# One core, 20,241 instructions: a top-k attention and two feed-forward blocks, replanned with other costs for landings, transposes and a shared port

## The chip, the cores and the metric

The kernel runs on one core of a Trainium2 chip. The metric is the device time of the program in microseconds. Three runs of the kernel before took 990.5, 990.6 and 991.75 us, so the median is 990.6 us. The execution that was profiled took 994.35 us, of which the span from the first to the last instruction is 992.6 us.

Five engines work side by side, each in the fixed order of its own instructions: PE (matrix products), DVE (VectorE), ACT (ScalarE), POOL (GpSimd) and SP, which does no arithmetic and issues all DMAs. An instruction that waits for a semaphore holds up everything behind it on its engine.

## The reference

```python
# attention: q, k, v are 4 x 8 x 576 x 64
scores = scale * np.matmul(q, k.transpose(0, 1, 3, 2))
kth = np.partition(scores, -32, axis=-1)[..., -32:-31]
scores = np.where(scores >= kth, scores, -1000000000.0)
scores = scores - np.max(scores, axis=-1, keepdims=True)
attn = np.exp(scores)
attn = attn / (np.sum(attn, axis=-1, keepdims=True) + 1e-09)
x = np.matmul(attn, v)            # as 2304 tokens x 512
# first block: w_in 512 x 2048, w_out 2048 x 512
h = x @ w_in
x = (h * (1.0 / (1.0 + np.exp(-1.702 * h)))) @ w_out
# second block: w1, w2 512 x 1024, w3 1024 x 1024, w_out 1024 x 512
out = ((x @ w1) * (x @ w2)) @ w3 @ w_out
```

The weights come in float64. Products are made in float16 with a high and a low half of each operand, three matmuls for one product (lines 789 to 791).

## The kernel before, in words

**Tiles and heads.** The 2304 tokens are 18 tiles of 128; a tile has 8 heads, so there are 144 heads. For one head PE makes the scores of 128 tokens with 576 keys into one of two score banks (`s_ps`, L1127, "S" below). DVE finds the 32 largest in four rounds of MAX8 (L1147) with three MATCH_REPLACE8 between them (L1150). ACT cuts (L1165, which also frees the score bank) and takes the exponential (L1168). ACT or POOL makes the high half ("a hi", L1174 or L1228), POOL or DVE the low half in two pieces ("a lor", 64 columns, L1177, and "a lo", 512 columns, L1180). A DMA transpose turns both halves into one of two `ats` buffers ("a T", L1183), and PE multiplies them with v ("av", L1195 and L1199).

**The two blocks.** After 8 heads a tile runs through `moe`: x is split and transposed ("x T", L1286), four products with w_in ("h"), tanh and gate (L1344 to L1356, "g"), split (L1313 to L1319) and transposed ("g T", L1359), products with w_out ("x2"), split and transposed ("x2 T", L1412), products with w1 and w2 ("a", "b"), their product p (L1461 or L1467), split and transposed ("p T", L1493), the product with w3 times w_out, made once at the start ("o"), and the store (L1509).

**The weights.** In the first 200 us 72 blocks of 512 KB are loaded (L483), rebuilt from their 64-bit words (ACT or POOL at L488, L493, L498 and L515, ACT at L503, DVE at L507), measured (PE at L551) and split (L598 to L630). K and v of each batch are prepared ahead of its tiles.

**What sets the order.** The code first records 5339 operations, each with one or more ways of doing it (an engine and a cost). A table of numbers (`PLAN`) gives each operation its rank and its way. `Order.run` goes through them by rank and emits each on its engine; it keeps modelled times only to choose which free buffer an operation gets. So the order on each engine, SP's DMA queue among them, is that of the table, and the semaphores follow from what each instruction reads and writes.

Buffers in the row of names below: `usb`, `tsb`, `psb` and `ysb` are rings in SBUF, `mm` are four PSUM banks, `w`, `win` and `wout` hold weights.

Of the kernel before, what the change touches and what calls it, by code (L numbers as in the profile page):

```python
# [21 lines left out]
P = 128  # L22
C = 512
# [14 lines left out]
class Order:  # L38
    GAP = {"T": 0.25, "V": 0.16, "A": 0.16, "G": 0.1, "D": 0.05, "N": 0.0}
    SAME = {"T": 0.0, "V": 0.12, "A": 0.12, "G": 0.1, "D": 0.25, "N": 0.0}  # L40
    DMA = 2.1
    COLD = ((50.0, 1.28), (100.0, 1.03))
# [99 lines left out]
    'c-jq@W1A(t0!2$nC8?w;N!3{A^f^6k_t-N%wr$(CZQHhO+qP}%oqPYm{;;3D)>af%(G{rJN@^vG;`8~HJW5_AzhWpr!3t5h!jv>hCdKomQUXe>66Oo_rBgzb'  # L142
    'cqKteRthWCl{!iRUqN4zl3U5A6jLhu8u{Az+WAT<6@9yv`btA(lrmMB>-*)~9C9>dy0Th1t6WhYDKC|`zE{d`<&W}3`R6OBwpaQp!<CWB4CTJ>r*DLRoU&ZG'
    'p*&VzD_@l#itVrEpXiVG=T<MMoz#WuGIhDST0QJP;TIuK)lYt;2%l73CB2eX$>7WEi%_DJvPuPCC0}i&sZvxa?yI6yRaz+-m8`ySU!0Od(G=5X`KaP3)s&jP'
    'TE1pVS0$)K`l5X~l_E+<Wr%O6Z<exEX{~he4OYe~)0DbOJ*9!tMCqZ-QRXXqlmp5^rKd99w@^8*oKRXQEq&dULCR!hnX<vR$+uV8ubfoQD;JcD%4OxMa?O`j'
    '4Oe5;C&~-o2Srh#`d!gg<R@x6)l!+C`xDh1Y6-Qb+DL7owp7!oq5cRpuUbsaqQ>|W{JGS!YH_u^zn;H|+EgvAlvg?^os@1$FQvEAPZ^*LR7NOclnKgAWuvmC'
    '!J!668cZy>NLjD!R3<6sd{caveDeyfQPwK!l)D8#DxZ{Z%It#Ml*P(+Wu<aU*{s}FR`^ym*wJ8DgMG>|<&1J&xvAVy?kNwHhssmsx$;JNr@U8&s1wwc>Kb*e'
    'x=vlMZculthtyN*dG(t5Ks8mVW>N!coSIWr{YD|z@A>nn`P9;C8MU0MsaO?iDz%haM-BSJ)M$Spe`~da+D+}Fj#6v;>#Ftrjs5-Afoev-uaMs#;vcHcP?xAn'
    ')y-;Ge~&`F{bT*d)Jy7ob%nZBy`p|o|EQX#Ylim5|5p9%|LTv_qBNxO!ct48<<|;mr9vu(R1V3ig%{4IW!GA0Z8fa9nx_S{f!ZK#lr~<Qs+9|=rd1EA6*5;_'
    't<BVC7hbF_*S2a0wL{ti?U7bTYg4#`)>nI|ebzQ<I}7jC4roZnx~)5U27QmZ-+$15S-q-8soDJb)rx90wXNFD-&q~4PFMS?1JvQ_ICYkKR6Xv$qyANiHb@<;'  # L150
    'j#1~T^VCV|Wd9ETUiGxvOl|IO@9(H~QKzVj{2SGq>PPjgde{HT|3Uqw{#H%R3Q4O4wG3JoEli8ia%vCNcj`~o)*Nk^I?_L0y{_I+Q)wAPVzp!~ueLy2sI3Xv'
    'rk&Rwsn68s>I?Oys%WYPwbWX)mZ@;lM!rUq8<p0|Hfq?YNuxA{>kX<sXxN}cEl;DQMl~Cq)y`>`w9DER?Va{s`=}{8(RDp3;0E#q78O~puhKW`S@bwPR?ng5'
    '*GmRU1*!+0YrnML+JD+Vjq9GCUJvRqdP0!`fn0&wfuZ_ZeYU<%57l$)QF=i=LeHy5>P2*^r_wX(ne;F{Tu;=q={fa6dR@Jx-a+rASJfNpZS=PKM15mmQeab{'
    'T#@>L%7F%fP%R>)Q%F~>x7J+i9MUbMpEg08rp*bNAF@>2s1??VYIQ@}Y3;RqTA`34S_!R^R$ptN^$!`WjnPJEW3}laGqhP+cdduE=l{iF`VsAv_C@=vnfi9^'
    'SjerAXWAQWnYJQieaLR@q;^<49&$qarm6a4Ekq9lD(Thqi(2+TdA+9IT(75h)cXed=`;18TC+eeeXu@9Z?AXOyXal@Zh8;BzdleOrH|9c>l5^8`Ye5}K3`v~'
    'uh!S->-DYrZvBjYF>obtBk;ONY%nocDELax5KI@$8r-X&&=2S*^#^(`BiYDp9MMk)jt1@ruIYCIw*yZD--;MUMx&rn+Ncw(9jq5TR^*|6PJgM>lt{xd;*32-'
    '{slnL3cf2+ESM=+Hh8GWt;RPSKWf~^m|*lZCL2mh(V!hH9xSY<1R4bz>%H|?TD*Q%zpFpf%j&HHWArWhWqp7?Jg_0~RsW;=jOs>1qq)(}$ZTXWqKpzo1>>Wh'
# [1410 lines left out]
```

## Time and profile before

| | |
|---|---|
| median of three runs | 990.6 us |
| profiled execution | 994.35 us, span 992.6 us |
| PE busy | 942.2 us (95%) |
| DVE busy | 901.7 us (91%) |
| POOL busy | 832.5 us (84%) |
| ACT busy | 730.0 us (74%) |
| DMA engines, mean busy share of queue 1 | 72.3% |

Busy time is the time in which an engine has at least one instruction under way. PE's matmuls overlap: a 128x512 matmul shows 0.38 us from start to end, and the next one starts 0.22 us after it. A wait that is shorter than this overlap leaves no idle time in the profile. A wait is put down to the releaser that came last.

### The profile page before, as it was taken

How to read it: one execution, taken by the hardware profiler on the slowest of the kernel's cores; microseconds unless marked ns; L12 is line 12 of the kernel's file. 1: busy time of each engine (PE TensorE's matmuls, PEld its weight loads, DVE VectorE, ACT ScalarE, POOL GpSimd, SP SyncE). 2: the span in 40 equal slices, each digit the busy share in tenths (PEclk: the TensorE clock that was granted, in tenths of full speed). 3: DMA queues.
4: the chain of work that ended last, by engine and by line, in shares of the span. 5: the costliest groups of instructions: out<-in, count | busy, mean ns of one | idle time of the engine just before them, and what ended most of it. 6: DMA issues, size and time to landing. Idle time of an engine off the chain costs nothing. (4 is left out here: it accounts for less than half of the span.)

```text
span 992.6 us, 20241 instructions
## 1 busy us (share of the span) xinstructions
PE 942.2 (95%) x6790; PEld 495.7 (50%) x6790; DVE 901.7 (91%) x1939; ACT 730.0 (74%) x1369; POOL 832.5 (84%) x1180
## 2 busy tenths in 40 slices
PE   5688879899999999999999999999999999999998
PEld 2445544445455555545555555545455555555544
DVE  6999999899999999999999999999999999999422
ACT  7999989896877787877688776776785775646241
POOL 6889999898899999999999999988897878757142
PEclk9699999999999999999999999999999999999999
DMA  9999988876788887767887868669666667555401
GB/s 322 291 280 291 277 179 191 173 135 131 122 149 151 155 156 136 134 130 152 146 158 139 147 129 147 121 127 165 127 126 134 113 118 117 111 90 102 99 11 33
DMA packets 398569, 149.37 MB, mean 150 GB/s; under 512 B 376576, under 2 KB 384768, under 8 KB 398464
## 3 DMA queue, kind: packets, MB, share of 16 engines
q1 hardware_dynamic: 398464, 148.07, 72.3%
q8 instruction: 53, 0.87, 0.4%
q14 instruction: 52, 0.43, 0.1%
HBM read 52.43 MB, written 4.72 MB: 58 GB/s over the span
## 5 line engine op out<-in xcount | busy, mean ns | idle before, releaser
L1147 DVE MAX8 m8s<-ysb 128x8 f32<-128x576 f32 x432 | 320.5, 752 | 5.7
L1150 DVE MATCH_REPLACE8 ysb<-m8s,ysb 128x576 f32<-128x576 f32 x288 | 213.6, 742 | 0.0
L1180 POOL TENSOR_TENSOR ysb<-ysb 128x512 f16<-128x512 f32 x141 | 163.8, 1166 | 0.3
L1165 ACT ACTIVATE ysb<-s_ps,m8s 128x576 f32<-128x576 f32 x144 | 106.7, 741 | 77.5 <-DVE m8s L1147 72.5
L789 PE MATMUL mm<-w,usb 128*128 128x512 f16 x388 | 147.1, 379 | 1.2 <-POOL usb L1319 1.0
L791 PE MATMUL mm<-w,usb 128*128 128x512 f16 x388 | 147.0, 379 | 0.0
L790 PE MATMUL mm<-w,usb 128*128 128x512 f16 x388 | 147.0, 379 | 0.0
L791 PEld LDWEIGHTS <-usb 128*128 128x128 f16 x912 | 89.1, 98 | 107.8
L789 PEld LDWEIGHTS <-usb 128*128 128x128 f16 x912 | 89.0, 98 | 100.2 <-issue 7.0
L1168 ACT ACTIVATE ysb<-ysb,nbs,asm 128x576 f32<-128x576 f32 x144 | 124.5, 867 | 17.0 <-DVE nbs L1157 8.5
L790 PEld LDWEIGHTS <-usb 128*128 128x128 f16 x912 | 89.1, 98 | 91.3 <-issue 2.1
L789 PE MATMUL mm<-wout,usb 128*128 128x512 f16 x304 | 115.3, 379 | 1.7 <-DMA usb<-usb 0.6
L791 PE MATMUL mm<-wout,usb 128*128 128x512 f16 x304 | 115.2, 379 | 0.0
L790 PE MATMUL mm<-wout,usb 128*128 128x512 f16 x304 | 115.2, 379 | 0.0
L1147 DVE MAX8 m8s<-s_ps 128x8 f32<-128x576 f32 x144 | 108.6, 754 | 6.2 <-PE s_ps L1127 3.4
L1150 DVE MATCH_REPLACE8 ysb<-m8s,s_ps 128x576 f32<-128x576 f32 x144 | 107.5, 747 | 0.0
L1127 PE MATMUL s_ps<-kts,qts 128*128 128x288 f16 (+1 forms) x640 | 96.4, 290 | 2.5 <-ACT ysb L1165 2.2
L789 PE MATMUL mm<-win,usb 128*128 128x512 f16 x220 | 83.5, 379 | 0.6 <-DMA usb<-usb 0.6
L791 PE MATMUL mm<-win,usb 128*128 128x512 f16 x220 | 83.4, 379 | 0.0
L790 PE MATMUL mm<-win,usb 128*128 128x512 f16 x220 | 83.4, 379 | 0.0
L1195 PE MATMUL mm<-v2s,ats 128*128 128x65 f16 (+1 forms) x1440 | 79.1, 194 | 3.4 <-DMA ats<-ysb 2.7
L1195 PEld LDWEIGHTS <-ats 128*128 128x128 f16 (+1 forms) x1440 | 73.5, 100 | 12.4 <-DMA ats<-ysb 3.8
(369 smaller groups left out, 2131.3 us busy)
## 6 DMA issues: line engine op xcount, KB each, us to landing
w<-in_moe_w_out_dram SPq DMA_DIRECT2D x24, 512.0 KB, 5.5
w<-in_moe_w_dram SPq DMA_DIRECT2D x22, 512.0 KB, 5.7
w<-in_moe_w_in_dram SPq DMA_DIRECT2D x16, 512.0 KB, 6.0
qts<-qts SPq DMA_DIRECT2D x34, 128.0 KB, 2.6
out_dram<-usb SPq DMA_DIRECT2D x17, 256.0 KB, 2.3
usb<-in_q_dram SPq DMA_DIRECT2D x15, 256.0 KB, 3.4
usb<-in_v_dram SPq DMA_DIRECT2D x11, 256.0 KB, 3.1
usb<-in_k_dram SPq DMA_DIRECT2D x10, 256.0 KB, 3.3
```

The lines of the kernel that those rows point to most:

```text
L789: nc.tensor.matmul(o, a[:, i, :], hi, start=(first and i == 0), stop=False)
L790: nc.tensor.matmul(o, a[:, i, :], lo, start=False, stop=False)
L791: nc.tensor.matmul(o, a[:, 4 + i, :], hi, start=False, stop=(last and i == 3))
L1127: nc.tensor.matmul(E["sp"][r : r + n, i], qe[q_][:, h, r : r + n], kt[:, j, i * HS : (i + 1) * HS], start=k_ == 0, stop=k_ == 1,)
L1147: nc.vector.max(out=E["m8"][:, 8 * i : 8 * i + 8], in_=E["sp"] if i == 0 else E["w"])
L1150: nc.vector.match_replace(out=two(E["w"]) if i == 0 else E["w"], in_to_replace=E["m8"][:, 8 * i : 8 * i + 8], in_values=E["sp"] if i == 0 ...
L1165: nc.scalar.activation(two(E["y"]), E["sp"], AF.Prelu, bias=E["m8"][:, TOPK - 1 : TOPK], scale=-1.0, alpha=1.0 / FAR)
L1168: nc.scalar.activation(E["y"], E["y"], AF.Exp, bias=E["nb"], scale=nesc)
L1180: return lambda: eng.tensor_tensor(hl()[:, S + SR : 2 * S], E["y"][:, 0:SM], hl()[:, 0:SM], op=ALU.subtract)
L1195: nc.tensor.matmul(heads_av()[r : r + n, j_, 0 : D + 1], at_, v2[:, j_, blk, D : P + 1], start=(i == 0), stop=(i == 8),)
```

## The change

The operations are the same. The planner's model gets later landings of all loads and transposes, a limit on what may be in flight when a transpose is issued (`ROOM`, counted in `UNITS`), a surcharge of 0.25 us on DVE operations that use the port shared with POOL (`TWO`), and slightly other costs for some POOL and PE operations. `PLAN` is new: other ranks, and for some operations another engine. The limit and the surcharge stand in the model; no instruction that waits for them is emitted. Lines behind the table move by 13 (L1183 becomes L1196).

```diff
     DMA = 2.1
+    ROOM = 2600
+    UNITS = {"w load": 512, "q load": 1024, "kv load": 512, "q swap": 128, "store": 128, "a T": 1152, "k T": 1152}
+    TWO = 0.25
     COLD = ((50.0, 1.28), (100.0, 1.03))
...
             if e == "G" or (e == "V" and fn in self.both):
-                cost += max(lock - now, 0.0)
+                cost += max(lock - now, 0.0) + (self.TWO if e == "V" else 0.0)
                 lock = now + cost
             o.eng, o.start = e, now
             free[e] = o.end = now + cost
             if e == "D":
+                units = self.UNITS.get(o.tag, 1024)
+                if o.tag[-2:] == " T":
+                    under = units
+                    for land, n in flight[:-13:-1]:
+                        under += n
+                        if under > self.ROOM:
+                            free[e] = o.end = max(o.end, land)
+                            break
                 moved = max(moved, now + 0.3) + o.data
                 o.end = max(o.end, moved) + o.lat
+                flight.append((o.end, units))
...
-            lat=3.05, data=0.55, after=last_of.get(("load", is_v)),
+            lat=3.5, data=0.55, after=last_of.get(("load", is_v)),
...
-        los = [("G", 1.118, f_lo(nc.gpsimd), 0.0), ("V", 0.68, od.two(f_lo(nc.vector)), 0.0)]
+        los = [("G", 1.13, f_lo(nc.gpsimd), 0.0), ("V", 0.68, od.two(f_lo(nc.vector)), 0.0)]
...
-            tr = [dma(1.35, due + 8, f_t, deps=[lo], env=E, acq=["at"], rel=["hl"], tag="a T", lat=1.6, data=1.42, after=last_of.get("a T"))]
+            tr = [dma(1.35, due + 8, f_t, deps=[lo], env=E, acq=["at"], rel=["hl"], tag="a T", lat=2.2, data=1.42, after=last_of.get("a T"))]
...
```

Operations that change engine, counted over the whole program: "a lor" on DVE 12 before, 3 after (POOL 132, 141); "a lo" on DVE 3, 1; "kvr lo" (L420 on DVE) 5, 1; evictions of PSUM on DVE at L1370, L1452 and L1470 together 9, 3; "nb" (L1157) on DVE 50, 57; "g" (L1350) on DVE 11, 15; the low halves at L1319 on DVE 3, 7; "p" (L1461) on DVE 6, 8. On ACT: "w low" (L488) 26, 31; "w sign" (L498) 39, 36. On PE one weight split more goes by the pair L610 and L611 (20 before, 21 after).

**SP's queue near 330 us.** The transposes of heads 38 and 39 are the second pair `ats<-ysb` of the piece before and the only pair of the piece after. Before:

```order
L1183 DMA_TRANSPOSE ats<-ysb 128x9x128 x2
L1359 DMA_TRANSPOSE tsb<-usb 128x8x128
L1493 DMA_TRANSPOSE tsb<-usb 128x8x128
L1183 DMA_TRANSPOSE ats<-ysb 128x9x128 x2
L976 DMA usb<-in_v_dram 128x2x256
L980 DMA rest<-in_v_dram 64x2x64 x2
L1509 DMA out_dram<-usb 128x512
L1493 DMA_TRANSPOSE tsb<-usb 128x8x128
```

After, on the same queue:

```order
L1506 DMA_TRANSPOSE tsb<-usb 128x8x128
L989 DMA usb<-in_k_dram 128x2x256
L993 DMA rest<-in_k_dram 64x2x64
L1372 DMA_TRANSPOSE usb<-usb 128x8x128
L1522 DMA out_dram<-usb 128x512
L1196 DMA_TRANSPOSE ats<-ysb 128x9x128 x2
L1372 DMA_TRANSPOSE usb<-usb 128x8x128
L1506 DMA_TRANSPOSE tsb<-usb 128x8x128
```

The load of v, which stood right behind the pair, has moved back by several DMAs; a store stands ahead of the pair now, and two transposes follow it.

**DVE near 766 us.** MAX8 and MATCH_REPLACE8 of heads 119 and 120, with the "a lor" of head 117 (L1177) between them. Before:

```order
L1150 MATCH_REPLACE ysb<-m8s,ysb 128x576
L1147 MAX m8s<-ysb 128x8
L1402 SCALAR_TENSOR_TENSOR usb<-mm_96,msm,usb 128x512
L1150 MATCH_REPLACE ysb<-m8s,ysb 128x576
L1082 RECIPROCAL asm<-asm 128x1
L1177 TENSOR_TENSOR ysb<-ysb 128x64
L1147 MAX m8s<-ysb 128x8
L1147 MAX m8s<-s_ps_93 128x8
```

After, on the same engine with the same heads:

```order
L1160 MAX m8s<-ysb 128x8
L1163 MATCH_REPLACE ysb<-m8s,ysb 128x576
L1170 TENSOR_SCALAR nbs<-m8s,asm 128x1
L1095 RECIPROCAL asm<-asm 128x1
L1415 SCALAR_TENSOR_TENSOR usb<-mm_97,msm,usb 128x512
L1160 MAX m8s<-ysb 128x8
L1163 MATCH_REPLACE ysb<-m8s,ysb 128x576
L1267 COPY xsb<-mm_95 128x130
L1160 MAX m8s<-ysb 128x8
L1160 MAX m8s<-s_ps_94 128x8
```

The "a lor" has gone to POOL; a small TENSOR_SCALAR ("nb") and a copy of a product stand on DVE in this stretch.

**ACT near 172 us, while the weights are prepared.** The row L1168 (after: L1181) is the exponential of the sixteenth head. Before:

```order
L617 ACTIVATE wout<-mm_97 128x512
L617 ACTIVATE w_72<-mm_96 128x512
L503 ACTIVATE mm_97<-tsb 128x512
L598 ACTIVATE win<-win,wsm 128x512
L617 ACTIVATE wout<-mm_95 128x512
L488 ACTIVATE w_72<-psb 128x512
L617 ACTIVATE wout<-mm_98 128x512
L488 ACTIVATE w_72<-w_72 128x512
L1168 ACTIVATE ysb<-ysb,nbs,asm 128x576
```

After:

```order
L1178 ACTIVATE ysb<-s_ps_93,m8s 128x576
L511 ACTIVATE wout<-w_72 128x512
L630 ACTIVATE wout<-mm_98 128x512
L516 ACTIVATE mm_97<-w_72 128x512
L501 ACTIVATE w_72<-psb 128x512
L1360 ACTIVATE usb<-usb 128x512
L516 ACTIVATE mm_95<-w_72 128x512
L611 ACTIVATE w_73<-wout,wsm 128x512
L1181 ACTIVATE ysb<-ysb,nbs,asm 128x576
```

The next head's cut (L1178) and a step of the first tile's gate (L1360) stand ahead of that exponential now, among the same kinds of weight steps.

## Rows read from the trace of the kernel before

**Rows 1.** Windows: busy us of each engine by stage, granted clock, DMA share, GB/s.

```profile
0.00:125.00 125.00, 96.56 (x640) 56.82 (x641) 112.23 (x248) 115.60 (x227) 108.00 (x167) 0.93 0.99 292
125.00:200.00 75.00, 64.52 (x471) 33.53 (x471) 69.04 (x165) 68.08 (x126) 68.39 (x98) 0.95 0.82 182
200.00:350.00 150.00, 146.03 (x1136) 76.13 (x1136) 146.91 (x331) 118.96 (x229) 137.43 (x206) 1.00 0.76 139
350.00:600.00 250.00, 248.28 (x1813) 130.76 (x1812) 243.87 (x520) 193.29 (x371) 237.56 (x334) 1.00 0.77 143
600.00:925.00 325.00, 323.13 (x2333) 166.39 (x2332) 308.65 (x641) 213.10 (x382) 261.06 (x356) 1.00 0.68 123
925.00:992.60 67.60, 63.66 (x404) 32.11 (x402) 21.01 (x38) 20.99 (x39) 20.10 (x23) 1.00 0.14 35
sum 992.60, PE 942.18 PEld 495.74 DVE 901.71 ACT 730.03 POOL 832.53; mean PE 157.03 PEld 82.62 DVE 150.29 ACT 121.67 POOL 138.76
```

**Rows 2.** Waits of PE from 200 us on: us in total, times, longest.

```profile
PE mm L1195 <- DMA ats<-ysb: 1.8, 5, 0.6
PE s_ps L1127 <- ACT ysb L1165: 1.3, 4, 0.5
PE mm L789 <- DMA usb<-usb: 1.2, 2, 0.6
PE mm L789 <- POOL usb L1319: 1.0, 1, 1.0
...
PE mm L789 <- DMA tsb<-usb: 0.8, 2, 0.6
```

**Rows 3.** Timeline of SP's issues, 332 to 336 us: start, us, engine, line.

```profile
332.93 2.85 SPq L1183 DMA_TRANSPOSE ats<-ysb  x2
335.88 1.23 SPq L976 DMA_DIRECT2D usb<-in_v_dram  x1
```

**Rows 4.** Timeline of PE at 338.9 us, idle time before in brackets.

```profile
338.90 0.22 PE L1195 MATMUL mm<-v2s,ats 128*64 128x65 f16 x1 [0.58 <-DMA ats<-ysb]
```

**Rows 5.** DMA issues: count, KB each where shown, median us to landing.

```profile
out_dram<-usb SPq DMA_DIRECT2D x17, 256.0 KB, 2.3
...
ats<-ysb SPq DMA_TRANSPOSE x142, 3.4
usb<-usb SPq DMA_TRANSPOSE x91, 3.2
```

**Rows 6.** Groups of DVE: count, busy us, mean ns of one, idle before.

```profile
L1157 DVE TENSOR_SCALAR nbs<-m8s,asm 128x1 f32<-128x1 f32 x50 | 13.1, 262 | 0.0
...
L1350 DVE SCALAR_TENSOR_TENSOR usb<-mm,wsm,usb 128x512 f32<-128x512 f32 x10 | 7.4, 739 | 0.0
L1177 DVE TENSOR_TENSOR ysb<-ysb 128x64 f16<-128x64 f32 x12 | 7.3, 612 | 0.0
...
L1180 DVE TENSOR_TENSOR ysb<-ysb 128x512 f16<-128x512 f32 x3 | 2.9, 1002 | 0.0
...
L1370 DVE TENSOR_SCALAR usb<-mm,wsm 128x512 f32<-128x512 f32 x2 | 1.5, 746 | 0.5 <-ACT usb L1344 0.5
...
L1319 DVE TENSOR_TENSOR usb<-psb,usb 128x512 f16<-128x512 f32 x2 | 1.4, 693 | 0.1
```

**Rows 7.** Timeline of DVE at 766 us: start, us, engine, line.

```profile
766.28 1.16 DVE L1177 TENSOR_TENSOR ysb<-ysb 128x64 f16<-128x64 f32 x1
```

**Rows 8.** Timeline of POOL at 766 us.

```profile
766.20 1.16 POOL L1180 TENSOR_TENSOR ysb<-ysb 128x512 f16<-128x512 f32 x1
```

**Rows 9.** Group of POOL.

```profile
L1177 POOL TENSOR_TENSOR ysb<-ysb 128x64 f16<-128x64 f32 x132 | 40.9, 312 | 10.9 <-ACT ysb L1174 7.1 <-DVE msm L534 1.2 <-ACT kvinv L1002 1.2
```

**Rows 10.** Groups of ACT.

```profile
L498 ACT ACTIVATE w<-w 128x512 f16<-128x512 f32 x12 | 9.4, 780 | 0.0
...
L488 ACT ACTIVATE win<-w 128x512 uint16<-128x512 uint8 x9 | 7.3, 806 | 0.0
```

**Rows 11.** Group of PE.

```profile
L610 PE MATMUL mm<-w,tsb 128*128 128x512 f32 x16 | 10.1, 716 | 2.6 <-POOL tsb L577 2.3
```

More of the change, by code (lines that the diff above doesn't have):

```diff
@@ L78, in run @@
         lock = moved = 0.0
+        flight = []
         for o in sorted(self.ops, key=lambda o: o.rank):
@@ L146 @@
[L146 to L157, printed above, removed]
@@ L509, in f_join @@
             )
-        ld = dma(0.5, due - 20, f_load, env=E, acq=keys, tag="w load", lat=2.5, data=1.62)
+        ld = dma(0.5, due - 20, f_load, env=E, acq=keys, tag="w load", lat=2.9, data=1.62)
         def f_low_g():
@@ L515, in f_low_g @@
             nc.gpsimd.tensor_scalar(low, b3, 1.0 / 32, -15.5 / 32, op0=ALU.mult, op1=ALU.add)
-        lo = op([("A", 0.637, f_low, 0.0), ("G", 0.77, f_low_g, 0.0)], due, deps=[ld], env=E, acq=[("blk", E, "w")], tag="w low")
-        sg = op([("A", 0.63, f_sign_a, 0.0), ("G", 0.75, f_sign, SIGN_G)], due, deps=[lo], tag="w sign")
+        lo = op([("A", 0.637, f_low, 0.0), ("G", 0.83, f_low_g, 0.0)], due, deps=[ld], env=E, acq=[("blk", E, "w")], tag="w low")
+        sg = op([("A", 0.63, f_sign_a, 0.0), ("G", 0.78, f_sign, SIGN_G)], due, deps=[lo], tag="w sign")
         mn = act(0.563, due, f_main, deps=[ld, sg], env=E, acq=["mm"], rel=out_, tag="w main")
@@ L588, in l2_scale @@
             return inv, sc, c
-        return inv, (turned, pool(0.35, due - 40, f_turn, deps=[c] + list(free), tag="w turn"), sc), c
+        return inv, (turned, pool(0.38, due - 40, f_turn, deps=[c] + list(free), tag="w turn"), sc), c
     def split(E, sc, dep, bank=False):
@@ L632, in split @@
             h = op(
-                [("A", 0.61, f_hi, 0.0), ("V", 0.4, od.two(f_hi_v), 0.0), ("G", 0.66, f_hi_g, 0.0)], 0.0, deps=[dep], env=E,
+                [("A", 0.61, f_hi, 0.0), ("V", 0.4, od.two(f_hi_v), 0.0), ("G", 0.69, f_hi_g, 0.0)], 0.0, deps=[dep], env=E,
                 acq=[("blk", E, "o")], tag="w hi",
@@ L644, in split @@
             return op(
-                [("V", 0.655, f_lo, 0.0), ("A", 0.475, f_lo_a, 0.0), ("G", 1.118, f_lo_g, 0.0), ("G", 1.9, f_lo_g2, 0.0), ("V", 0.66, od.two(f_lo_v2), 0.0)], 0.0,
+                [("V", 0.655, f_lo, 0.0), ("A", 0.475, f_lo_a, 0.0), ("G", 1.13, f_lo_g, 0.0), ("G", 1.9, f_lo_g2, 0.0), ("V", 0.66, od.two(f_lo_v2), 0.0)], 0.0,
                 deps=[E["in"], pre], env=E, rel=["mm", ("blk", E, "w")], tag="w lo",
@@ L791, in part @@
                 nc.tensor.matmul(o, a[:, 4 + i, :], hi, start=False, stop=(last and i == 3))
-        x = pe(1.295, due, lambda: part(0, 2), deps=deps, acq=acq, tag=tag)
-        return pe(1.295, due, lambda: part(2, 4), deps=[x], rel=rel, tag=tag)
+        x = pe(1.3, due, lambda: part(0, 2), deps=deps, acq=acq, tag=tag)
+        return pe(1.3, due, lambda: part(2, 4), deps=[x], rel=rel, tag=tag)
     ready = {}
@@ L1043, in kv_prep @@
         last_of["k T"] = dma(
-            3.9, due, f_t, deps=[m, r], env=E, rel=["h", "kr"], tag="k T", lat=1.2, data=2.7, after=last_of.get("k T")
+            3.9, due, f_t, deps=[m, r], env=E, rel=["h", "kr"], tag="k T", lat=1.8, data=2.7, after=last_of.get("k T")
         )
@@ L1078, in f_swap @@
             nc.sync.dma_start(E["qb"][D:P], E["qa"][0:D])
-        ld = dma(0.55 * len(parts(t)), due - 6, f_load, deps=[tail_of.get(t - 3)], env=E, acq=[stage], tag="q load", lat=3.0, data=0.4)
+        ld = dma(0.55 * len(parts(t)), due - 6, f_load, deps=[tail_of.get(t - 3)], env=E, acq=[stage], tag="q load", lat=3.5, data=0.4)
         a = act(0.707, due, f_abs, deps=[ld], env=E, acq=["h"], tag="q abs")
@@ L1305, in tile_end @@
             return
-        X["xt"] = dma(1.32, due, f_t, deps=[s], env=X, acq=["t"], rel=["h"], tag="x T", lat=1.6, data=1.42, after=last_of.get(("g T", t - 2)))
+        X["xt"] = dma(1.32, due, f_t, deps=[s], env=X, acq=["t"], rel=["h"], tag="x T", lat=2.2, data=1.42, after=last_of.get(("g T", t - 2)))
     def hi_lo(due, E, src, deps, rel, acq=(), tag="", wait=2.0, wait_hi=2.0):
@@ L1321, in hi_lo @@
         a = op([("A", 0.515, h_a, 0.0), ("V", 0.37, od.two(h_v), wait_hi)], due, deps=deps, env=E, acq=["h"], tag=tag + "hi")
-        return op([("G", 1.118, l(nc.gpsimd), 0.0), ("V", 0.66, od.two(l(nc.vector)), wait)], due, deps=[a], env=E, rel=rel, tag=tag + "lo")
+        return op([("G", 1.13, l(nc.gpsimd), 0.0), ("V", 0.66, od.two(l(nc.vector)), wait)], due, deps=[a], env=E, rel=rel, tag=tag + "lo")
     def moe(t, X):
```

208 lines of the change are left out of this document (110 added, 98 removed).

## The prediction

> **What bounds the kernel now.** I read the windows by stage first, then the waits of PE, then the timelines of SP and PE around one late transpose, and last the groups of DVE, POOL and ACT from which the change takes work or to which it gives some.
>
> By stage [rows 1] PE is idle for 125.00 - 96.56 = 28.4 us up to 125 us and 75.00 - 64.52 = 10.5 us up to 200 us, 38.9 us together. There the DMA engines are full (share 0.99 up to 125 us) and ACT and DVE nearly so (115.6 and 112.2 of 125): the weights come in and are rebuilt. From 200 us PE is idle for 4.0, 1.7 and 1.9 us in the next three stages, 7.6 us in 725, and 3.9 us at the very end. The granted clock is 1.00 (the 2.4 GHz level) in all of them, so no clock is to be won there. DVE is nearly as full: 146.9 of 150, 243.9 of 250, 308.7 of 325. After 925 us it has almost nothing left (21.0 of 67.6), and PE works off what has piled up. So the end is PE's: its work plus the waits that it meets, and DVE feeds it with hardly any lead.
>
> The waits of PE from 200 us on [rows 2] are few. Nine are for transposes that had not landed (1.8 + 1.2 + 0.8 = 3.8 us), four for a score bank (1.3), one for a low half from POOL (1.0). Matmuls of 0.38 us start 0.22 us apart, so every wait behind one hides some 0.16 us more than its idle time shows. The nine then cost 3.8 + 9 x 0.16 = 5.2 us, the other five 2.3 + 5 x 0.16 = 3.1 us, 8.3 us in all. One of the nine can be followed: two `ats` transposes are issued back to back from 332.93 us, the load of v follows at 335.88 [rows 3], and PE, with 0.58 us of visible idle, starts on the first only at 338.90 [rows 4], 6.0 us after the issue. The median of that transpose is 3.4 us [rows 5]. So it is not the usual landing that PE waits for but the late one, in company of other DMAs.
>
> **The change part by part.** The sum is made against the profiled execution, 994.35 us (span 992.6 and 1.75 around it). That is 3.75 us above the median of the three runs, and I take these off at the end.
>
> Landings. SP's queue is ordered anew, and the consumers on PE with it. At the place just followed the load of v no longer stands behind the pair; two transposes do. What I can price is the waits: 5.2 us is the most that can go, 0 the least if each finds a successor. The model that places the consumers now counts on more time for every landing, which covers some late ones but not one of 6 us. I take two thirds, -3.3 us. The instructions and the bytes of the queue stay as they were, so SP has no more to issue.
>
> DVE. Off it go nine "a lor" at 0.612, two "a lo" at 1.002 and six evictions at about 0.746 [rows 6]: 5.5 + 2.0 + 4.5 = 12.0 us. On it come seven "nb" at 0.262, four gates at 0.739, four low halves at 0.693 and two products that I price like these: 1.8 + 3.0 + 2.8 + 1.4 = 9.0 us. That is -3.0 us; swaps that I don't price by rows (casts, four small halves of k and v, two weight splits) go mostly the same way, and as an estimate they bring it to -8 at the most. "a lor" is dear on DVE for a reason that the trace shows: at 766.28 us [rows 7] it took 1.16 us and ended with POOL's "a lo", which had begun at 766.20 and also took 1.16 [rows 8]. On POOL it takes 0.312 [rows 9], nine of them 2.8 us, where POOL has 12.6, 12.4 and 63.9 us of idle in the three stages from 200 to 925 us [rows 1]. DVE's work stands beside PE's; on the path it counts only where PE waits for a score bank or for something late behind DVE, which is the 3.1 us above. Half of that goes: -1.5 us; bounds 0 and the -8 of a kernel that DVE paces.
>
> The Trainium skill (SBUF — State Buffer, section "SBUF: two separate sides") says that VectorE and GpSimd take a shared port pair as an exclusive lock, that an instruction of VectorE with two SBUF inputs is among those that contend, and that the loser waits for the whole instruction. The trace agrees at 766 us. It speaks against part of this change: the four low halves put on DVE have two SBUF inputs, and by the rule each could stand for up to another 1.16 us, 4.6 us of DVE in all, which would eat the -3.0 us. The three that DVE has now took 0.693 us on average [rows 6] and show no such wait; I keep the row's price.
>
> Weights. Five "w low" go to ACT, at 0.806 us, and three "w sign" leave it, at 0.780 [rows 10]: 4.0 - 2.3 = +1.7 us on an engine that has 9.4 us of idle up to 125 us, most of it before the first loads land, and 6.9 in the next stage [rows 1]. The first loads and PE's order of the first 200 us are nearly unchanged. Which wait ends last there changes from step to step; I take 0, and a tenth of PE's 38.9 us to either side as bounds, -4 and +4.
>
> PE. One more weight split goes by the pair of L610 and L611. A 128x512 product in float32 shows as two records, so the sixteen are eight operations, 10.1 / 8 = 1.26 us each [rows 11]; with its partner, and one matmul of L837 less, +1.2 us. PE is the engine that sets the end, so it counts in full.
>
> The tail stays: from the products of heads 140 and 141 to the last one PE has the same work, with a "turn" or a product moved by one place.
>
> Sum: -3.3 - 1.5 + 0 + 1.2 = -3.6 us. 994.35 - 3.6 = 990.75 in a profiled execution; less 3.75, 987.0 us.
>
> **The rivals.**
>
> DVE sets the pace of the heads up to 913 us, and PE only seems to, because it is fed just in time. For it: DVE at 97.5% from 350 to 600 us and score-bank waits at all. Against: 16 us of idle on DVE from 600 to 925 us, where PE has 1.9 [rows 1]. Then DVE's -8 us come off nearly whole, and part of the landings, -2.3: -8 - 2.3 + 1.2 = -9.1, 981.5 us.
>
> The landing waits move and do not go. For it: the late landing seen was 2.6 us over the median, and a plan that adds a little to all of them leaves it late; also the limit in flight stands in the model alone, and the piece of the queue after still has `ats` pairs back to back with other transposes. Then only the DVE term and PE's extra work are left: -1.5 + 1.2 = -0.3, 990.3 us.
>
> The Trainium skill (Advanced Engine Details and Errata, section "X-Bar Transpose (TRN2)") says that transpose DMAs are as fast as regular ones. By that, later landings would be needless, and this rival would be the result. The trace disagrees by a little: 256 KB of `usb` land in 3.2 us as a transpose, in 2.3 us as a store [rows 5].
>
> Slower: ACT in the first 200 us. The place is the weight stage, where the next cut and a gate step now stand ahead of the sixteenth head's exponential, and five "w low" more are on ACT. If POOL, which is given three "w sign" for them, does not hand its blocks on sooner, ACT's 5 x 0.806 = 4.0 us delay the joins and so PE. Then 990.6 + 4.0 + 1.2 - 1.5 = 994.3 us. It decides when PE's idle time up to 200 us grows from 38.9 to over 42. For it: ACT at 92% in the first 125 us; against: ACT's 6.9 us of room from 125 to 200 [rows 1], and that PE's backlog at 925 us shows that work not done early is done late without loss only if PE has room, which it has not.
>
> **How the numbers follow.** The forecast, 987.0, has 0.45, with a range of its own from 983.5 to 989 (all 8.3 us of waits gone, or a third of them, and +1.2). DVE's pace, 981.5, has 0.12. No change, 990.3, has 0.21. ACT's stage, 994.3, has 0.22. A difference under 0.2%, 2 us, can't be told from none: 988.6 to 992.6 us is "same". Nearly all of the forecast and DVE's pace lie below, the third case within, the fourth above: faster 0.57, same 0.21, slower 0.22. The range reaches from 980 (DVE's pace with a little more) to 994.5: outside lie some 0.05 below and half of the slower case above.
>
> **What would show it.** Right: in the windows PE's idle time from 200 to 925 us falls from 7.6 to 3 or 4 us, the waits of PE for `ats`, `usb` and `tsb` from 3.8 to under 2 us, the longest landing of an `ats` pair followed by a load is gone, and DVE's busy time falls by 3 to 8 us; up to 200 us PE's idle stays within 4 us of 38.9. Wrong: those waits reappear under other names with the same sum (no change); PE's idle up to 200 us is over 42 us, with waits for ACT or for the joins at L507 (slower); or PE's idle time from 200 us on hardly falls, and still the time falls by more than 6 us, which would mean that most waits were the hidden kind.

## The result, and the profile after

The kernel after takes 982.84 us (median; the runs lie between 981.7 and 984.76), the kernel before beside it 990.93 us: a ratio of 0.9919, 95% interval 0.9901 to 0.9938, or -8.0 us (-9.8 to -6.1). Forecast were 987.0 us, -3.6. The profiled execution has a span of 981.7 us (before 992.6), PE busy 935.6 us (942.2), DVE 892.2 (901.7), ACT 733.0 (730.0), POOL 826.0 (832.5). Lines above 150 have moved by 13: L1195 is now L1208, L789 is L802.

The windows by stage, with the columns of [rows 1]:

```profile
0.00:125.00 125.00, 96.86 (x671) 58.38 (x672) 112.55 (x257) 116.78 (x224) 108.29 (x171) 0.90 1.03 291
125.00:200.00 75.00, 65.06 (x476) 34.40 (x475) 74.47 (x179) 73.97 (x143) 71.64 (x101) 1.00 0.89 198
200.00:350.00 150.00, 147.63 (x1161) 76.84 (x1162) 146.98 (x327) 119.62 (x226) 138.43 (x210) 1.00 0.75 138
350.00:600.00 250.00, 248.63 (x1796) 131.17 (x1795) 244.17 (x527) 199.24 (x381) 234.23 (x325) 1.00 0.79 144
600.00:925.00 325.00, 324.58 (x2402) 168.46 (x2401) 298.59 (x616) 204.91 (x372) 261.42 (x370) 1.00 0.66 123
925.00:981.70 56.70, 52.83 (x292) 25.76 (x290) 15.45 (x26) 18.46 (x33) 12.01 (x14) 1.00 0.10 29
```

From 200 to 925 us PE is now idle for 2.4 + 1.4 + 0.4 = 4.2 us, where it was 7.6. Up to 200 us its idle time is 28.1 + 9.9 = 38.1 us, as good as the 38.9 of before, and yet something has changed there: from 125 to 200 us DVE is busy for 74.47 of 75 us (69.04 before), ACT for 73.97 (68.08), POOL for 71.64 (68.39), and the granted clock is 1.00 (0.95). Up to 125 us the clock is no better than before (0.90, was 0.93). Between the two profiles the span falls by 10.9 us, and PE's idle time over the whole span by 4.3 us only (50.4, now 46.1); the other 6.6 us are busy time, which a slow clock and waits too short to be seen make longer.

The waits of PE from 200 us on, all that the view shows (compare [rows 2]):

```profile
PE s_ps L1140 <- ACT ysb L1178: 1.8, 4, 1.3
PE mm L1208 <- DMA ats<-ysb: 1.3, 2, 0.7
PE mm L802 <- DMA usb<-usb: 0.6, 2, 0.4
PE mm L931 <- DVE wsm L928: 0.2, 1, 0.2
```

Nine waits for a landing, 3.8 us, have become four, 1.9 us; those for a score bank have not shrunk (1.3, now 1.8). The landings themselves are no shorter. The `ats` transposes issued from 200 us on, 126 in either kernel, before and then after:

```profile
DMA to landing us min/median/max: 3.2/3.4/5.9
```

```profile
DMA to landing us min/median/max: 3.2/3.4/5.7
```

Over 4.5 us took 12 of them before and 15 after. At the pair of heads 38 and 39, whose landings took 5.9 and 5.3 us before and take 4.6 and 5.1 us after, PE now begins 6.8 us after the issue and does not wait, where it began 6.0 us after it and waited [rows 3, rows 4]:

```profile
325.67 3.54 SPq L1196 DMA_TRANSPOSE ats<-ysb  x2
```

```profile
332.49 0.22 PE L1208 MATMUL mm<-v2s,ats 128*64 128x65 f16 x1
```

The groups of DVE that answer to [rows 6]:

```profile
L1332 DVE TENSOR_TENSOR usb<-usb 128x512 f16<-128x512 f32 x4 | 3.1, 772 | 0.4 <-ACT usb L1326 0.3
L1332 DVE TENSOR_TENSOR usb<-psb,usb 128x512 f16<-128x512 f32 x4 | 2.7, 687 | 0.1
...
L1190 DVE TENSOR_TENSOR ysb<-ysb 128x64 f16<-128x64 f32 x3 | 1.2, 384 | 0.7 <-ACT ysb L1187 0.7
```

By the trace DVE has eight low halves at this line, not the seven that were counted for the change: five more than before, not four.

**How far PE has come.** Idle time doesn't say how early a stage is through. So for single score products I take the start and subtract the time of all PE work ahead of it in that kernel's order, at one price for each kind of operation (0.2155 us for a 128x512 matmul in float16, 0.49 for a score product). What is left is what PE has lost by then: idle time, waits too short to be seen, and slow clock. The starts are read like this, for head 20, before and then after (duration in ns, first and last start):

```profile
L1127 PE MATMUL s_ps<-kts,qts x4: 286/286/297, 203.1 to 203.5; 128*128 128x288 f16 x4
```

```profile
L1140 PE MATMUL s_ps<-kts,qts x4: 286/286/286, 195.5 to 195.9; 128*128 128x288 f16 x4
```

The order after gets there 7.6 us sooner, with as much work ahead to within 0.5 us. The table holds the us lost, for the two kernels and for those experiments that are read by it (heads are counted from 0):

| order up to 200 us | before | before | before | after | after | after | after | after, 5 w low on POOL |
|---|---|---|---|---|---|---|---|---|
| order from there | before | before (e3) | after (e2) | after | before (e1) | before from 255 us (e5) | after, a lor on DVE (e4) | after (e6) |
| head 10 | 44.3 | 42.5 | 41.8 | 44.4 | 41.7 | 43.3 | 42.4 | 43.8 |
| head 12 | 49.1 | 46.1 | 45.8 | 46.1 | 43.5 | 45.0 | 44.3 | 48.9 |
| head 20 | 66.8 | 63.0 | 61.7 | 58.8 | 56.7 | 58.7 | 58.2 | 61.0 |
| head 30 | 70.6 | 67.3 | 65.4 | 62.4 | 63.9 | 67.2 | 61.6 | 64.7 |
| head 96 | 77.5 | 74.9 | 69.6 | 67.8 | 68.8 | 73.3 | 66.6 | 70.1 |
| head 143 | 81.3 | 80.0 | 71.8 | 69.6 | 74.5 | 77.3 | 70.4 | 71.3 |

Between the two profiles 8.0 of 11.7 us lie ahead of head 20. But the profile of before was the worst of its kind: e2 and e3, which run the same operations on the same engines in the same order up to there, had lost 61.7 and 63.0, not 66.8. The middle of three against the middle of four is 63.0 - 58.45 = 4.6 us, and the extra weight split, which the order before never does, takes some 0.85 us of it back: some 3.7 us are left. Four later runs (described below) that share an order up to there, read in the same way, had lost 62.0 us (order before, e7) and 56.4, 59.0 and 56.7 us (order after, e8, e11 and e12), which would make it some 3.4.

### The profile page after: what moved, and what is told of

Its sections match the earlier page's. It is cut to its first block, busy times and chain, and to the rows that moved or that the text cites. A ratio compares the mean times of both kernels' runs of the same rounds, so it can differ in the third digit from the quotient of the medians.

```text
span 981.7 us, 20248 instructions
## 1 busy us (share of the span) xinstructions
PE 935.6 (95%) x6792; PEld 495.0 (50%) x6792; DVE 892.2 (91%) x1927; ACT 733.0 (75%) x1374; POOL 826.0 (84%) x1187
## 5 line engine op out<-in xcount | busy, mean ns | idle before, releaser
L1178 ACT ACTIVATE ysb<-s_ps,m8s 128x576 f32<-128x576 f32 x144 | 106.7, 741 | 82.1 <-DVE m8s L1160 62.0
L804 PEld LDWEIGHTS <-usb 128*128 128x128 f16 x876 | 85.7, 98 | 103.7 <-issue 0.5
L802 PE MATMUL mm<-w,usb 128*128 128x512 f16 x355 | 134.7, 379 | 0.6 <-DMA usb<-usb 0.6
L1181 ACT ACTIVATE ysb<-ysb,nbs,asm 128x576 f32<-128x576 f32 x144 | 124.5, 867 | 13.4 <-POOL nbs L1170 10.1
L804 PE MATMUL mm<-w,usb 128*128 128x512 f16 x355 | 134.5, 379 | 0.0
L803 PE MATMUL mm<-w,usb 128*128 128x512 f16 x355 | 134.5, 379 | 0.0
L802 PEld LDWEIGHTS <-usb 128*128 128x128 f16 x876 | 85.6, 98 | 92.3 <-issue 4.4
L803 PEld LDWEIGHTS <-usb 128*128 128x128 f16 x876 | 85.7, 98 | 89.5 <-issue 3.5
L802 PE MATMUL mm<-wout,usb 128*128 128x512 f16 x293 | 111.5, 381 | 2.3 <-ACT wout L630 0.9
L804 PE MATMUL mm<-wout,usb 128*128 128x512 f16 x293 | 111.3, 380 | 0.0
L803 PE MATMUL mm<-wout,usb 128*128 128x512 f16 x293 | 111.3, 380 | 0.0
L802 PE MATMUL mm<-win,usb 128*128 128x512 f16 x228 | 86.5, 379 | 0.1
L804 PE MATMUL mm<-win,usb 128*128 128x512 f16 x228 | 86.4, 379 | 0.0
L803 PE MATMUL mm<-win,usb 128*128 128x512 f16 x228 | 86.4, 379 | 0.0
L1208 PE MATMUL mm<-v2s,ats 128*128 128x65 f16 (+1 forms) x1440 | 78.5, 194 | 3.7 <-DMA ats<-ysb 3.0
L1208 PEld LDWEIGHTS <-ats 128*128 128x128 f16 (+1 forms) x1440 | 73.3, 100 | 14.0 <-DMA ats<-ysb 4.7
```

What stands on the lines that cost most here:

```text
L802: nc.tensor.matmul(o, a[:, i, :], hi, start=(first and i == 0), stop=False)
L803: nc.tensor.matmul(o, a[:, i, :], lo, start=False, stop=False)
L804: nc.tensor.matmul(o, a[:, 4 + i, :], hi, start=False, stop=(last and i == 3))
L1178: nc.scalar.activation(two(E["y"]), E["sp"], AF.Prelu, bias=E["m8"][:, TOPK - 1 : TOPK], scale=-1.0, alpha=1.0 / FAR)
L1181: nc.scalar.activation(E["y"], E["y"], AF.Exp, bias=E["nb"], scale=nesc)
L1208: nc.tensor.matmul(heads_av()[r : r + n, j_, 0 : D + 1], at_, v2[:, j_, blk, D : P + 1], start=(i == 0), stop=(i == 8),)
```

## The experiments

Each ratio is to runs of the kernel before made beside it; a difference in us is (ratio - 1) x 990.9. Where `PLAN` or the costs were edited, the edit is told in words. In e1 to e4 line numbers are 6 lower than in the kernel after. In e7 (against before) and e8 (against after) they are 2 higher, behind the edit 5; in e10 they are 1 higher.

**e1_early.**

```diff
-PLAN: order and engines of the kernel after, 5339 operations
+PLAN: operations 1 to 1340 as in the kernel after (up to head 20),
+      the others in the order and on the engines of the kernel before
```

> The kernel after up to operation 1340 (the score product of head 20, about 200 us), the kernel before's order and engine choices from there on. Theory W (most of the 8.1 us come from the stage in which the weights are rebuilt, up to 200 us, and hold to the end because PE has no room later to catch up): the stage's 8 us come off, 983 us (982 to 985). Theory L (the forecast: landings and DVE's relief after 200 us, the weight stage worth nothing): what is changed after 200 us is not in it, so 990 us (989 to 991.5).

Measured: 989.49 us, 0.9976 (0.9961 to 0.9990), -2.4 us. Theory W is wrong in this form: the stage is done as early as in the kernel after (56.7 lost at head 20), and then 7.2 us go between heads 20 and 30, where the kernel after loses 3.6.

**e2_late.**

```diff
+PLAN: operations 1 to 1340 as in the kernel before, the others as in the kernel after
```

> The mirror: the kernel before up to operation 1340, the kernel after from there on. Theory W: only what was gained after 200 us is left, about 3 us by the two profiles: 988 us (986.5 to 989.5). Theory L: all of the gain, 983 us (982 to 984.5). If the two halves only work together, both this and its mirror stay near 990.

Measured: 984.88 us, 0.9949 (0.9935 to 0.9963), -5.1 us. Between W's 988 and L's 983, nearer to L: most of the gain is made after 200 us. The landing waits of PE from 200 us on are down to one, 0.6 us. What the order after gives besides in the first 200 us is the rest, 8.0 - 5.1 = 2.9 us, between 0.6 and 5.2 by the two intervals taken together. The mirror e1_early gave 2.4 us for it.

**e3_constants.**

```diff
-PLAN: the table of the kernel after
+PLAN: the table of the kernel before, with the new costs
```

> The new costs, the landings, the limit in flight and the surcharge, with the table of the kernel before. Only the choice among free buffers can differ. Both theories: 990.9 us, within 1 us. A rival (the buffers picked by the new landings take the waits away): 988 us or less.

Measured: 992.61 us, 1.0018 (1.0009 to 1.0027), +1.8 us. Neither theory, and not the rival: buffers picked by the new costs make the old order a little slower. Its landing waits from 200 us on are 3.1 (`tsb`), 2.5 (`ats`) and 0.9 us (`usb`).

**e4_lor_on_dve.**

```diff
-a lor: 3 on DVE, 141 on POOL; a lo: 1 on DVE
+a lor: 12 on DVE, 132 on POOL; a lo: 3 on DVE
```

> The kernel after, with the low rests and low halves of the attention weights (a lor, a lo) on the engines where the kernel before had them: twelve a lor and three a lo on DVE again, some 7 us of DVE's busy time, in the order of the kernel after. Theory W: DVE's relief is worth little, 983 to 984 us. Theory L by its own term: +1.5 us, 984.3. The rival in which DVE paces the heads: nearly all of the 7 us come back, 988 us or more.

Measured: 984.50 us, 0.9942 (0.9930 to 0.9954), 2.3 us over the kernel after, with some 2 us to either side. DVE's busy time rose by 4 us only, not by 7 (896.4 us up to 975 us, 892.2 in the kernel after). One reason is that an "a lor" and an "a lo" are cheaper here than in the kernel before (0.612 and 1.002): the two groups grew by 4.7 and 1.3 us. The first group, and PE's waits for a score bank, of which there are six now and were four (1.8 us):

```profile
L1184 DVE TENSOR_TENSOR ysb<-ysb 128x64 f16<-128x64 f32 x12 | 5.9, 494 | 0.3 <-ACT ysb L1181 0.2
```

```profile
PE s_ps L1134 <- ACT ysb L1172: 2.7, 6, 1.3
```

By the table the loss from head 20 to head 143 is 12.2 against 10.8 us: +1.4, all of it behind head 96, where most of these operations stand. So these 4 us are worth some 1 to 2 us, the size of the forecast's term. The runs alone, with 0.1 to 4.5 us, do not rule out that all 4 come back, as they would with a pacing DVE; the table speaks against it.

**e5_early_255.**

```diff
-PLAN: the cut of e1_early at operation 1340
+PLAN: the same cut at operation 1660 (head 30)
```

> The cut of e1_early moved from operation 1340 (200 us) to 1660 (255 us, the score product of head 30), a place where the two orders differ by three operations only. By the profile of e1_early PE lost 2 to 3 us right behind the seam (heads 20 to 24), which neither kernel loses there. Theory S (the weight stage is worth 4 to 5 us and the seam of e1_early ate half): 986.5 us (985.5 to 987.5). Theory L (the stage is worth 2.4 us as measured there): 988.5 us and more.

Measured: 990.84 us, 0.9992 (0.9979 to 1.0004), no gain that can be told. Theory S is wrong about the seam: this one is worse. At 255 us one transpose of the old order is late for PE. The wait in the stretch around it, and the matmul that ends it:

```profile
PE mm L802 <- DMA usb<-usb: 3.0, 1, 3.0
```

```profile
255.22 0.59 PE L802 MATMUL mm<-w,usb 128*128 128x512 f16 x1 [2.98 <-DMA usb<-usb]
```

Up to head 20 the stage is as early as in the kernel after (58.7), at head 30 all of that is gone (67.2, as in e3). Part of it is the clock, which was granted at 0.50, the 1.2 GHz level, behind the wait:

```profile
256.00:258.00 2.00, 2.00 (x7) 0.78 (x6) 0.00 (x0) 0.00 (x0) 2.00 (x2) 0.50 1.45 94
```

Here time won before a stretch that was laid out for later arrivals was not handed on to the end.

**e6_wlow_on_pool.**

```diff
-w low of 5 weight blocks: ("A", L501)
+w low of the same 5 blocks: ("G", L528), at 59, 85, 97, 102 and 119 us
```

> The kernel after, with five of its w low between 65 and 115 us back on POOL, as in the kernel before, and all else as it is. If the engine choices carry the gain of the weight stage (POOL's queue set the pace of the kernel before at 141 and 187 us): five times 0.8 us on POOL, the stage is 2 to 4 us longer, 985 to 987 us. If the order carries it and ACT is as full as POOL: within 1 us of the kernel after, 982 to 984 us.

Measured: 985.85 us, 0.9944 (0.9932 to 0.9957), 2.5 us over the kernel after, as for the engine choices expected, though with some 2 us to either side. The place is the one where the old order loses too: from head 10 to head 12 it lost 5.1 us, after 1.7, before 4.8. The last of the five is the first row here, POOL around 120 us (on ACT, in the kernel after, it began at 115.97):

```profile
119.28 0.77 POOL L528 TENSOR_SCALAR win<-w 128x512 uint16<-128x512 uint8 x1
120.12 0.79 POOL L528 TENSOR_SCALAR w<-tsb 128x512 uint16<-128x512 uint8 x1
120.97 0.77 POOL L506 TENSOR_SCALAR win<-w 128x512 bf16<-128x512 f32 x1
```

The "w sign" of the same block (L506) stands behind it and another low word, and DVE's join (L520) waits for it:

```profile
121.78 0.69 DVE L520 SCALAR_TENSOR_TENSOR win<-mm,win 128x512 uint32<-128x512 uint32 x1 [1.05 <-POOL win L506]
```

PE from 105 to 130 us waits for such joins, first here, then in the kernel after:

```profile
PE mm L564 <- DVE win L520: 1.9, 2, 1.3
```

```profile
PE mm L564 <- DVE win L520: 0.2, 1, 0.2
```

**e7_before_disturbed** and **e8_after_disturbed.** The same edit in both kernels:

```diff
         def f_t():
+            if t >= 3:
+                nc.sync.dma_start(out=dummy[n % 2], in_=q[0, 0, 0:P, 0:8])
             nc.sync.dma_start_transpose(out=E["at"], in_=hl())
```

> The kernel before with one small load (4 KB into a spare tile) put on SP's queue ahead of each transpose of attention weights from the fourth tile on, 120 in all. An issue takes 0.57 us on SP, so each transpose, and what stands behind it, is issued 0.57 to 1.1 us later. Theory L (PE waits for late landings, with little room): a third or more of the heads now wait, 5 us longer or more, 996 us and up. The rival (the landings have room enough, the gain after 200 us is DVE's relief): 991 to 993 us.

> The same 120 loads in the kernel after. Theory L (its consumers stand later, so there is room for a late landing): it loses at most half of what the kernel before loses by them, 984 to 986 us. The rival (as in e7_before_disturbed, or both equally short of room): it loses the same, within 1 us.

Measured: e7 1006.16 us, 1.0165 (1.0143 to 1.0186), +16.3 us; e8 992.23 us, 1.0005 (0.9996 to 1.0014), which is 8.5 us over the kernel after. The kernel before lost as theory L has it, 996 us and up; the kernel after lost more than the 984 to 986 us of theory L, but about half of what the other lost (8.5 of 16.3), the bound that it named. The last two heads have no such transpose, so the loads are 118, not 120. The rival, the same loss in both, is out. SP's queue in e7, and under it the landings (the last figure is the median in us; in e8 they are the same):

```profile
331.43 0.63 SPq L1187 DMA_DIRECT2D dummy<-in_q_dram  x1
332.22 1.41 SPq L1188 DMA_TRANSPOSE ats<-ysb  x1
```

```profile
ats<-ysb SPq DMA_TRANSPOSE x142, 3.3
dummy<-in_q_dram SPq DMA_DIRECT2D x118, 4.0 KB, 2.1
usb<-usb SPq DMA_TRANSPOSE x91, 3.2
```

A landing takes no longer than before [rows 5]; it is the issue that comes later. The waits of PE from 200 us on, in e7 and then in e8:

```profile
PE mm L1200 <- DMA ats<-ysb: 7.0, 13, 1.3
PE mm L791 <- DMA usb<-usb: 5.7, 7, 1.6
...
PE mm L791 <- DMA tsb<-usb: 1.5, 2, 1.3
```

```profile
PE mm L1213 <- DMA ats<-ysb: 5.8, 6, 2.1
PE mm L804 <- DMA usb<-usb: 2.1, 3, 0.9
...
PE mm L804 <- DMA tsb<-usb: 0.2, 1, 0.2
```

22 waits of 14.2 us against 10 of 8.1. With 0.16 us more for each, as in the prediction, they are 12.5 us more than before in e7 and 7.2 us more than in the kernel after in e8, most of what each lost: the consumers in the order after have more room for a late transpose, but not for every one.

**e9_before_actq** and **e10_after_actq.** In both kernels:

```diff
-            nc.sync.dma_start(E[sk]..., src[b, ...])      # and E["rest"], L989 to L993
+            eng = nc.scalar if b >= 1 else nc.sync
+            eng.dma_start(E[sk]..., src[b, ...])
...
-                nc.sync.dma_start(qst()[r : r + n], q[...])
+                (nc.scalar if t >= 3 else nc.sync).dma_start(qst()[r : r + n], q[...])
...
-            nc.sync.dma_start(out[t * P : (t + 1) * P, :], Eo["f"])
+            nc.scalar.dma_start(out[t * P : (t + 1) * P, :], Eo["f"])
```

> The kernel before with its stores, its q loads from the fourth tile on and its k and v loads from the second batch on issued by ACT instead of SP, at the same places of the order: some 90 issues of 0.57 us that SP no longer has between the transposes; the bytes stay. The mirror of e7_before_disturbed. Theory L (what PE waits for is transposes that SP issues late): the waits for landings shrink, 985 to 988 us. The rival (the DMA engines themselves are late, SP's queue does not matter): 990 to 992 us, or more if ACT's instructions now wait for buffers.

> The same in the kernel after. Theory L: it has little landing wait left, so it gains less than the kernel before does by the same edit, 0 to 2 us: 981 to 983 us. The rival: as in e9_before_actq, no gain, or a loss where ACT waits.

Measured: e9 1017.14 us, 1.0265 (1.0239 to 1.0291), +26.3 us; e10 1011.84 us, 1.0212 (1.0186 to 1.0237), +21.0. Both theories missed what the edit does: on ACT a load is issued no earlier than ACT's own work ahead of it allows. A load of v in e10, and the operation that reads it, both on ACT:

```profile
411.63 0.39 ACTq L990 DMA_DIRECT2D usb<-in_v_dram  x1
412.06 0.63 ACTq L994 DMA_DIRECT2D rest<-in_v_dram  x1
...
414.63 0.72 ACT L998 ACTIVATE v2s<-usb,nbs 128x512 f16<-128x512 f32 x1 [1.51 <-DMA usb<-in_v_dram]
```

In the kernel after SP issued a load of v at 382.71 us and ACT read it at 388.37, 5.7 us later, without a wait. Such waits of ACT for loads come to 18 us in e10 from 200 us on (the longest 4.2), and to as much in e9; the kernel after has none. They pass on to PE, which waits 5.7 us for L998, once 3.4. Before 200 us e10 has one more, of 5.0 us, for which PE waits 4.8. So these two say nothing of SP's queue.

**e11_plan_only.**

```diff
-costs, ROOM, UNITS, TWO of the kernel after
+the code of the kernel before, with the table of the kernel after
```

> The new table alone: the code and the costs of the kernel before with the order and engine choices of the kernel after. Only which free buffer an operation gets differs from the kernel after. e3_constants (the new costs with the old table) was 1.7 us slower than the kernel before. If the buffers picked by the new landings only hurt an order that was not made with them: 984 us or more here. If buffers hardly matter: 982.5 to 983.5 us.

Measured: 984.17 us, 0.9922 (0.9905 to 0.9939), -7.7 us, where the kernel after has -8.0. The median lies just in the first case, but the ratio can't be told from the kernel after: the gain is in the order and the engines, and the buffers hardly matter to it.

**e12_store_on_act.**

```diff
-            nc.sync.dma_start(out[t * P : (t + 1) * P, :], Eo["f"])
+            nc.scalar.dma_start(out[t * P : (t + 1) * P, :], Eo["f"])
```

> The kernel after with only the 18 stores of the output issued by ACT, which makes most of the rows that they store; the loads are on SP as in the kernel after, ahead of their readers. It takes 18 issues of 0.57 us off SP and, by the trace of the kernel after, three waits of SP for ACT at the store (16.3 us in all), behind which transposes stand. If the loss of e9_before_actq and e10_after_actq came from the loads, which have readers on ACT a few instructions later, it is gone here, and theory L gives a small gain: 981 to 983 us. If any DMA on a second queue costs time: 985 us or more.

Measured: 983.87 us, 0.9924 (0.9904 to 0.9944), the kernel after within the interval. A second queue costs nothing that can be told here, so what cost e9 and e10 their time were the loads. There is no gain that can be told either.

## Why the prediction was right or wrong, step by step

**The number.** The time fell by 8.0 us, more than twice the 3.6 that were forecast. 982.84 us lies below the range that the forecast had for itself, 983.5 to 989, and nearest to the 981.5 of the rival in which DVE sets the pace; only the outer range, 980 to 994.5, holds it. So the time fell as forecast, but the sum of the terms was too small.

**After 200 us: right in place, and as a sum in size.** The steps on landings and on DVE gave -3.3 - 1.5 = -4.8 us; the late part alone measured -5.1 (e2, -6.4 to -3.7). Landing waits fell as foretold, from 3.8 to 1.9 us, PE's idle time from 7.6 to 4.2; five waits fewer at the 0.16 us that each hides make it -1.9 - 0.8 = -2.7 for the landings. The cause is the one that the step named: the consumers on PE stand later, the landings are as late as they were. e7 and e8 show that room by itself: the same delay of the issues costs the order after half of what it costs the order before. The step on DVE is not borne out in its own terms. Of the 3.1 us of other waits that it halved, 2.8 are left (2.0 us seen, five waits): the one for a low half is gone, those for a score bank are not. Two waits for ACT, which the prediction left out of its count, are gone as well, 1.0 us seen and 1.3 in all:

```profile
PE mm L661 <- ACT win L655: 0.8, 1, 0.8
...
PE mm L789 <- ACT usb L1353: 0.2, 1, 0.2
```

By the waits it is thus -2.7 - 0.3 - 1.3 = -4.3 us, and that -4.8 came so near to -5.1 is in part luck: what the score-bank waits did not give, others gave. That DVE's relief is worth 1 to 2 us is what e4 says, within wide bounds. DVE's busy time fell by 9.5 us, a little past the 3 to 8 that were named.

**Up to 200 us: the term that was mis-sized.** It was "I take 0" for the weights, with bounds of 4 us to either side, and +1.2 for PE's extra split. The bounds did not go into the forecast's own range either. Measured is about -2.9 for both (the kernel after against e2) and -3.7 by the table, so some -4 in place of the 0 if the split is taken out, at the edge of the bounds. The step looked at PE's idle time, which hardly changed, and at the five "w low" as a load on ACT. In the kernel before PE waits from 125 to 200 us for joins and for a tile from POOL most of all:

```profile
PE mm L551 <- DVE w L507: 2.5, 4, 1.8
PE mm L610 <- POOL tsb L577: 2.3, 2, 1.8
```

The five "w low" stand between 59 and 119 us. From 60 to 125 us ACT is as full before as after (63.5 and 63.1 of 65 us), so they pushed other work out of this stretch; behind it, where ACT had room, its 68.1 us of 75 became 74.0. With the five back on POOL the joins come late and 2.5 us return, with 2 us to either side (e6); DVE and ACT are then still nearly as full from 125 to 200 us (73.8 and 71.9 us), so most of that is the work of the order and not of the five. The rest of the -4 was not taken apart: order and engines of this stage were only tried together.

**The extra split cost no +1.2.** Its pairs became cheaper. The float32 products, before [rows 11] with the two groups that were not shown there, and after:

```profile
L610 PE MATMUL mm<-win,tsb 128*128 128x512 f32 x16 | 9.4, 674 | 0.7 <-ACT xsb L1251 0.4 <-ACT usb L1353 0.2
L610 PE MATMUL mm<-wout,tsb 128*128 128x512 f32 x8 | 5.2, 736 | 0.2 <-DVE wout L614 0.2
```

```profile
L623 PE MATMUL mm<-win,tsb 128*128 128x512 f32 x18 | 9.6, 613 | 1.1 <-DVE w L627 0.8 <-ACT xsb L1264 0.4
L623 PE MATMUL mm<-wout,tsb 128*128 128x512 f32 x12 | 6.4, 617 | 0.0
L623 PE MATMUL mm<-w,tsb 128*128 128x512 f32 x12 | 6.4, 614 | 0.0
```

40 records took 10.1 + 9.4 + 5.2 = 24.7 us, 42 take 22.4. In e2 and e3, with the order before in this stage, the 40 took 23.3 us: 1.4 of the 24.7 belong to the profile of before alone. Before, PE's clock fell behind stalls in this stage; the windows of before (column of the granted clock third from the end), and then of after:

```profile
145.00:150.00 5.00, 4.44 (x38) 2.35 (x37) 4.48 (x12) 3.47 (x8) 4.92 (x8) 0.79 0.44 91
...
185.00:192.00 7.00, 5.01 (x16) 1.84 (x14) 5.12 (x16) 3.91 (x8) 6.62 (x11) 0.76 0.84 172
```

```profile
145.00:150.00 5.00, 5.00 (x19) 2.21 (x20) 5.00 (x11) 5.00 (x10) 4.92 (x9) 1.00 0.89 169
...
185.00:192.00 7.00, 7.00 (x60) 3.78 (x58) 7.00 (x17) 7.00 (x16) 6.71 (x11) 1.00 0.67 143
```

The dip at 145 us is there with the old order in e2, e3 and e7 too (0.93 from 125 to 150 us); with the order after the clock was 1.00 there in e1, e4, e5, e8, e11 and e12, but 0.94 in e6. Of the two with waits for loads, e9 (order before) has its dip earlier, 0.93 from 100 to 125 us, and e10 (order after) 0.80 from 125 to 150. The dip at 187 us came in the profile of before alone: e2 and e3 have 1.00 from 175 to 200 us.

**The rivals.** DVE's pace asked for -8 - 2.3 = -10.3 us, nearly all of it after 200 us (no "a lor" stands on DVE ahead of 510 us); the late part gave -5.1 (e2), and 4 us put back on DVE cost 1.4 by the table (e4). So it does not hold, near as its number came. That the landing waits only move is out: there are fewer of them, and the order after takes a delay of the issues at half the price (e8). ACT's stage, the slower one, was wrong in sign: ACT did get its work, from 68.1 to 74.0 us in 75, and PE did not wait more for it. That POOL handed its blocks on sooner, as this rival itself allowed, is shown for the five blocks of e6. The rule of the Trainium skill (SBUF — State Buffer, section "SBUF: two separate sides") was weighed against the low halves on DVE. It bit once: of eight, seven took 0.68 to 0.72 us, and one, at 903.34 us, 0.99 beside POOL's "a lo" (902.58 to 903.78 us), 0.3 us more and not 1.16. But all eight stand behind 894 us, where POOL has little left to do, so they hardly test it. The four that hold the long one:

```profile
L1332 DVE TENSOR_TENSOR usb<-usb x4: 691/706/986, 894.2 to 938.2; 128x512 f16<-128x512 f32 x4
```

**The base.** Taking 3.75 us off for the profiled execution was right on the whole, and e2 and e3 show where most of them lay: in the weight stage, where they had lost 61.7 and 63.0 us at head 20 and the profile of before 66.8.

## What to carry to other kernels

Where several engines hand work to each other and all are over 90% busy, idle time of the last one need not tell what a stage is worth (here it stayed at 38 us while the stage gave some 4): look which queue stands in front of the operation that joins them, and give that stage a range with the sign open, and a price. A wait for a transfer is a matter of room in the order, so test it with a small delay of every issue: how much a kernel loses by it tells how much room it has. Time won early was kept here only where the order behind it was made for it; and before two profiles are subtracted, see how far each is from its median, and in which stage.

## What the hardware showed that was not expected

One small DMA of 4 KB, with some 0.58 us of SP's queue for each of 118, cost 16.3 us in one order and 8.5 in the other, while the median landing of the transposes behind it grew no longer (3.3 us).

Stalls of a few us were paid twice: in the two windows shown that hold them the granted clock was 0.79 and 0.76, and float32 matmuls of 0.59 us took up to 1.2, the 1.2 GHz level. In e5 a wait of 2.98 us was followed by a granted clock of 0.50 from 256 to 258 us.

The loads of q, k and v, issued by ACT at the same place of the order, left readers on ACT waiting for up to 5.0 us. In the kernel after, where SP issues them, no reader on ACT waits for them from 200 us on.
